# Decay totals of ten units taken from the last row of k's factor by small transfers, in an RWKV-6 and SwiGLU kernel

## The chip, the core and the metric

The kernel runs on one core of a Trainium2 chip. The metric is the device time of one execution in microseconds. Five engines work side by side, each through its own list of instructions in order: TensorE (PE in the profile, its weight loads shown as PEld), VectorE (DVE), ScalarE (ACT), GpSimd (POOL) and SyncE (SP), which here does nothing but issue transfers. Semaphores hold an instruction back until what it needs is there; whatever stands behind it on the same engine waits with it.

## What is computed

A recurrence over time with a state of 48 x 48 for each of 8 heads and 4 sequences, and a gated feed-forward layer on its output:

```python
for t in range(S):                                   # S = 768, D = 48
    cur = einsum('bhd,bhe->bhde', u * k[t], v[t])
    y[t] = einsum('bhd,bhde->bhe', r[t], state + cur)
    state = w[t][:, :, :, None] * state + einsum('bhd,bhe->bhde', k[t], v[t])
...
xn = x / sqrt(mean(x * x) + 1e-6) * rms_g            # x: 3072 tokens x 384
out = (silu(xn @ w_gate) * (xn @ w_val)) @ w_out     # 384 -> 1536 -> 384
```

All inputs are fp32, and so is the output of 3072 x 384.

## The kernel before

**Units.** Time is cut into six superblocks n = 0 to 5 of 128 steps (L), and in each the four sequences j = 0 to 3 are handled apart: a unit is a pair (n, j), 128 steps on the partitions and 8 heads x 48 values along a row. For a unit the recurrence becomes matrix products: with c the running sum of ln w within the superblock, r is multiplied by exp(c before the step), k by exp(-c after the step), the products r k (masked to earlier steps) give the part inside the superblock, and the state carries the rest. At the end of the unit the state is multiplied by the decay of the whole superblock, exp(the sum of ln w over all 128 steps). These numbers are called the decay totals here; there are 8 x 48 of them to a unit, and they are needed with the value index on the partitions, two heads to a column (`wcol`, 128 x 4 x 2).

**Steps of a unit that matter here**, each a function of the kernel:

- `ln` (ACT) makes ln w. `cs_mm` (PE) multiplies it by a triangular mask: the sums before each step go to a PSUM bank, `ps_au` or `ps_av`, columns 4 to 387. Four more matmuls (line 420) with ln w as the weights and a column of ones as the moving operand put the totals, already turned onto the partitions, into columns 0 to 3 of the same bank.
- `cs_add` (DVE) adds ln w for the sums after each step, into `ps_bu` or `ps_bv`.
- `exp_r` (ACT) takes the exponential of the first bank in place, totals included; `exp_k` (ACT) that of the second with the sign turned, into an SBUF tile `ek` (fp32, four buffers).
- `w_tot` (DVE, line 451) reads the four columns from PSUM and spreads them into `wcol`. `r_mul` (DVE) and `k_mul` (POOL, line 461, from superblock 2 on) multiply r and k by their factors into `rk`.
- `rk_tr` turns `rk` by a transposing transfer on SP's queue into `rkT`; `q_mm`, `y_mm` and `st_mm` (PE) use it; `st_new` (DVE, lines 536 and 537) adds the old state to the new products and multiplies by `wcol`.

Then come `x_add`, `x_sq`, `x_rstd`, `xn_mul`, `xn_pe` and `xn_out`, which normalise the 512 tokens of the superblock, and the feed-forward layer: twelve pairs `gate_mm` and `val_mm` (PE, line 626), each with `silu` (ACT) and `h_mul` (DVE, line 658), and four `o_mm` (PE, line 672) with `o_out` and `out_dma`. The feed-forward work of superblock n - 1 is interleaved with the recurrence of superblock n.

**What sets the order.** One table, `ORDER`, names every step of the program in one line of text, as function.n.j. The program is written out in that order, so each engine runs its share of the table strictly in that order, SP's transfers too. Buffers come in rings: PSUM in two banks `a` (gate, and the sums of `cs_mm`), two banks `b` (val, and `cs_add`) and four banks `q`. A `val_mm` therefore waits until the `h_mul` two places earlier has read its bank. SP issues, in one list, the loads of r, k, v and w, the transposing transfers of `rk_tr`, and the stores of the output.

Of the kernel before, what the change touches and what calls it, by code (L numbers as in the profile page):

```python
# [68 lines left out]
q_mask_o.2.3 st_mm.2.3 load_k.3.0 q_mask_o.2.2 q_mask_e.2.3 val_mm.1.11 q_mask_e.2.2 val_mm.1.10 bonus_v.2.3 y_mm.2.3
silu.1.11 y_mm.2.2 ln.3.0 h_mul.1.11 h_mul.1.10 x_rstd.2.1 x_add.2.2 ln.3.1 val_mm.1.8 ln.3.3 h_mul.1.8 cs_mm.3.0  # L70
load_r.3.0 x_sq.2.2 xn_mul.2.0 cast_v.3.2 cs_add.3.0 x_add.2.3 exp_k.3.0 x_sq.2.3 o_mm.1.0 cs_mm.3.1 xn_pe.2.0
exp_r.3.0 ln.3.2 x_rstd.2.2 o_mm.1.1 st_new.2.3 load_r.3.1 out_dma.0.3 w_tot.3.0 r_mul.3.0 xn_mul.2.1 k_mul.3.0
xn_mul.2.2 cs_add.3.1 exp_k.3.1 xn_pe.2.2 cs_mm.3.3 x_rstd.2.3 o_out.1.0 exp_r.3.1 bonus_mul.3.1 xn_out.2.2 xn_mul.2.3
o_mm.1.3 w_tot.3.1 xn_pe.2.3 o_out.1.1 cs_add.3.3 r_mul.3.1 load_k.3.2 load_r.3.3 xn_pe.2.1 xn_out.2.0 exp_r.3.3
exp_k.3.3 cs_mm.3.2 xn_out.2.3 o_mm.1.2 load_r.3.2 k_mul.3.1 w_tot.3.3 rk_tr.3.0 r_mul.3.3 cs_add.3.2 out_dma.1.0
xn_out.2.1 load_v.3.0 exp_r.3.2 gate_mm.2.5 exp_k.3.2 r_mul.3.2 w_tot.3.2 val_mm.2.0 gate_mm.2.0 bonus_mul.3.0
bonus_mul.3.2 k_mul.3.2 o_out.1.3 bonus_sum.3.0 silu.2.5 rk_tr.3.1 load_k.3.3 o_out.1.2 q_mm.3.0 silu.2.0 q_mask_e.3.0
val_mm.2.1 bonus_v.3.0 h_mul.2.0 gate_mm.2.1 load_w.4.1 load_v.3.1 load_k.4.3 st_mm.3.2 k_mul.3.3 q_copy_o.3.0
silu.2.1 rk_tr.3.2 load_v.4.0 rk_tr.3.3 val_mm.2.5 gate_mm.2.11 load_k.4.0 bonus_sum.3.1 cast_v.3.0 out_dma.1.1
load_v.3.3 load_w.5.2 q_mask_e.3.1 q_copy_o.3.1 gate_mm.2.2 silu.2.11 h_mul.2.5 val_mm.2.2 h_mul.2.1 load_w.4.0  # L80
# [12 lines left out]
rk_tr.4.0 xn_out.3.3 cs_add.4.3 load_k.5.3 o_mm.2.3 exp_r.4.3 xn_out.3.2 cs_add.4.2 bonus_mul.4.3 r_mul.4.3 w_tot.4.3
exp_k.4.3 exp_r.4.2 rk_tr.4.1 o_out.2.3 exp_k.4.2 load_v.4.2 val_mm.3.1 gate_mm.3.6 bonus_sum.4.0 k_mul.4.3 r_mul.4.2
st_mm.4.0 w_tot.4.2 load_r.5.3 load_k.5.0 val_mm.3.0 o_out.2.2 silu.3.6 st_new.4.0 k_mul.4.2 gate_mm.3.1 q_mm.4.0
cast_v.4.2 out_dma.2.2 bonus_sum.4.3 silu.3.1 gate_mm.3.0 q_copy_o.4.0 silu.3.0 h_mul.3.1 q_copy_o.4.1 gate_mm.3.3
val_mm.3.6 gate_mm.3.8 rk_tr.4.3 q_mask_e.4.0 h_mul.3.0 h_mul.3.6 st_mm.4.1 bonus_v.4.0 q_mask_e.4.1 q_mask_o.4.0
# [5 lines left out]
h_mul.3.10 silu.3.7 val_mm.3.2 gate_mm.3.5 h_mul.3.2 load_k.5.2 gate_mm.3.11 q_mask_o.4.2 y_mm.4.2 cast_v.4.3
xn_mul.4.1 val_mm.3.7 silu.3.5 bonus_mul.5.0 x_add.4.2 silu.3.11 ln.5.1 y_mm.4.3 h_mul.3.7 val_mm.3.11 x_add.4.3
load_v.5.3 x_sq.4.2 xn_tr.4.0 h_mul.3.11 x_sq.4.3 xn_tr.4.1 val_mm.3.5 st_mm.4.3 h_mul.3.5 x_rstd.4.2 cs_mm.5.1
cs_add.5.1 ln.5.2 xn_mul.4.2 x_rstd.4.3 o_mm.3.2 o_out.3.2 cs_mm.5.2 xn_tr.4.2 exp_k.5.1 cs_add.5.2 exp_r.5.1 o_mm.3.0
xn_mul.4.3 r_mul.5.1 ln.5.3 ln.5.0 xn_tr.4.3 cs_mm.5.0 st_new.4.3 exp_r.5.2 cast_v.5.3 exp_k.5.2 o_mm.3.1 out_dma.3.2
cs_add.5.0 out_dma.2.3 r_mul.5.2 exp_r.5.0 cs_mm.5.3 r_mul.5.0 st_mm.4.2 exp_k.5.0 cs_add.5.3 exp_r.5.3 o_mm.3.3
bonus_mul.5.1 xn_gain.4.0 xn_gain.4.2 xn_gain.4.1 k_mul.5.0 r_mul.5.3 exp_k.5.3 o_out.3.1 out_dma.2.1 o_out.3.0
gate_mm.4.0 val_mm.4.1 gate_mm.4.1 val_mm.4.0 bonus_sum.5.1 st_new.4.2 k_mul.5.1 k_mul.5.3 silu.4.0 load_v.5.0  # L110
rk_tr.5.0 silu.4.1 h_mul.4.0 gate_mm.4.3 gate_mm.4.2 rk_tr.5.1 silu.4.3 val_mm.4.2 bonus_sum.5.0 k_mul.5.2 gate_mm.4.4
silu.4.2 bonus_v.5.1 o_out.3.3 cast_v.5.0 h_mul.4.1 val_mm.4.3 q_mm.5.0 gate_mm.4.6 h_mul.4.2 bonus_mul.5.2 h_mul.4.3
# [19 lines left out]
def kernel(  # L132
# [18 lines left out]
    SB = B  # L151
# [573 lines left out]
```

## Time and profile before

| what | us |
|---|---|
| median of 3 runs | 201.49 |
| the three runs | 199.88, 201.49, 202.73 |
| the profiled execution, its own time | 200.28 |
| span of that execution in the profile | 198.6 |
| PE busy | 191.9 |
| DVE busy | 151.4 |
| ACT busy | 137.3 |
| POOL busy | 125.2 |

The times named below are microseconds from the start of the span. That execution took 1.7 us more than its span, which runs from the first instruction to the last. In rows of the timeline, the first number is the start, the second the duration, and a bracket tells of idle time before the row and of who ended it. An operation's line tells which function it comes from; `ps_au` and the like are PSUM banks. The granted clock of TensorE was 1.00 over the span.

### The profile page before, as it was taken

The page shows a single profiled execution, that of the slowest core. Times are in us where ns is not written, and L with a number is a line of the kernel's source. Part 1 is how long each engine was busy: PE and PEld are TensorE (multiplying, and loading weights), DVE is VectorE, ACT ScalarE, POOL GpSimd, SP SyncE. Part 2 cuts the span into 40 slices and gives each one's busy share as a digit, 9 for nine tenths or more (in the row PEclk, how much of TensorE's full clock was granted, in tenths as well). Part 3 has the DMA queues.
Part 4 walks back from the last instruction along what each step waited for, and adds up shares of the span by engine and source line. Part 5 has one row for each costly group of instructions (what it writes and reads, how often), then busy time and mean ns, then how long its engine had stood idle before and what let it go on. Part 6 is the DMA issues. An engine that isn't in the chain of part 4 may idle for free.

```text
span 198.6 us, 4409 instructions
## 1 busy us (share of the span) xinstructions
PE 191.9 (97%) x1577; PEld 113.9 (57%) x1577; DVE 151.4 (76%) x290; ACT 137.3 (69%) x279; POOL 125.2 (63%) x184
## 2 busy tenths in 40 slices
PE   7979998999999999999999999999999999999994
PEld 3556574465665565665556665556655565555562
DVE  6358989989998799987889989987887973173611
ACT  4399989579979569958559959399786683164300
POOL 5378993189399687899939899867686851000000
PEclk9999999999999999999999999999999999999999
DMA  6999999999999998999899879995499012032012
GB/s 153 268 235 176 183 220 203 214 180 211 179 195 224 206 196 196 236 198 207 193 195 225 188 171 204 204 183 107 138 187 208 0 25 60 6 112 83 0 59 101
DMA packets 121566, 32.41 MB, mean 163 GB/s; under 512 B 116420, under 2 KB 120392, under 8 KB 121544
## 3 DMA queue, kind: packets, MB, share of 16 engines
q1 hardware_dynamic: 119504, 28.58, 67.3%
q0 software_dynamic: 2032, 3.54, 10.0%
q8 instruction: 12, 0.20, 0.4%
q14 instruction: 10, 0.08, 0.1%
q10 hardware_dynamic: 8, 0.00, 0.0%
HBM read 25.96 MB, written 4.72 MB: 154 GB/s over the span
## 4 chain that ended last, share of the span: by engine, by line
PE 72%; SPq 18%; DMA 6%; POOL 2%; issue 1%; ACT 0%; POOLq 0%
SPq L248 16%; PE ps_av L626 10%; PE ps_bu L626 10%; PE ps_bv L626 10%; PE ps_au L626 10%; PE ps_qv L672 7%; PE ps_qz L672 7%; PE ps_qu L672 5%; PE ps_qx L672 4%; DMA wo_sb<-in_moe_w_out_dram 4%; DMA vt<-in_v_dram 3%; SPq L261 2%; PE ps_qz L502 1%; PE ps_qx L552 1%; PE ps_av L417 1%
## 5 line engine op out<-in xcount | busy, mean ns | idle before, releaser
L672 PEld LDWEIGHTS <-ht 128*128 128x128 bf16 x300 | 28.2, 98 | 17.0 <-issue 0.5
L626 PEld LDWEIGHTS <-wg_sb 128*128 128x128 bf16 x216 | 23.1, 114 | 19.7 <-DMA wg_sb<-in_moe_w_gate_dram 0.7
L626 PEld LDWEIGHTS <-wv_sb 128*128 128x128 bf16 x216 | 22.8, 114 | 19.0 <-DMA wv_sb<-in_moe_w_val_dram 1.0
L658 DVE TENSOR_TENSOR ht<-ps_bv,sg 128x512 bf16<-128x512 f32 x35 | 24.0, 686 | 10.1 <-PE ps_bv L626 9.2
L235 ACT ACTIVATE sg<-ps_av 128x512 bf16<-128x512 f32 x37 | 22.0, 595 | 12.3 <-PE ps_av L626 12.0
L626 PE MATMUL ps_av<-xnt,wg_sb 128*128 128x512 bf16 x111 | 30.1, 380 | 0.0
L626 PE MATMUL ps_bu<-xnt,wv_sb 128*128 128x512 bf16 x111 | 30.1, 380 | 0.0
L658 DVE TENSOR_TENSOR ht<-ps_bu,sg 128x512 bf16<-128x512 f32 x37 | 25.4, 686 | 6.0 <-PE ps_bu L626 5.2
L626 PE MATMUL ps_bv<-xnt,wv_sb 128*128 128x512 bf16 x105 | 28.5, 380 | 0.6 <-DMA wv_sb<-in_moe_w_val_dram 0.5
L626 PE MATMUL ps_au<-xnt,wg_sb 128*128 128x512 bf16 x105 | 28.5, 380 | 0.2 <-DMA wg_sb<-in_moe_w_gate_dram 0.2
L235 ACT ACTIVATE sg<-ps_au 128x512 bf16<-128x512 f32 x35 | 21.0, 599 | 10.8 <-PE ps_au L626 9.0
L467 POOL TENSOR_TENSOR ruk<-rt,kt 128x384 f32<-128x384 f32 x24 | 24.1, 1003 | 6.6 <-DMA kt<-in_k_dram 4.8
L468 POOL TENSOR_TENSOR ruk<-ruk,u_bc 128x384 f32<-128x384 f32 x24 | 24.4, 1017 | 1.9
L520 POOL TENSOR_SCALAR_AFFINE_SELECT qts<-qts 128x512 bf16<-128x512 bf16 x20 | 12.9, 653 | 15.1 <-ACT qts L513 14.6
L477 POOL TENSOR_TENSOR ydiag<-vt,diag 128x384 f32<-128x384 f32 x24 | 19.9, 833 | 1.0 <-DVE rk L461 0.5
L461 POOL TENSOR_TENSOR rk<-kt,ek 128x384 bf16<-128x384 f32 x16 | 15.9, 1007 | 2.3 <-ACT ek L235 2.3
L672 PE MATMUL ps_qv<-wo_sb,ht 128*128 128x384 bf16 (+1 forms) x96 | 15.0, 306 | 0.0
L672 PE MATMUL ps_qz<-wo_sb,ht 128*128 128x384 bf16 x84 | 14.8, 326 | 0.0
L233 ACT ACT_TABLE_LOAD x10 | 12.8, 1283 | 1.8 <-PEq L709 1.6
L235 ACT ACTIVATE lw<-wt 128x384 bf16<-128x384 f32 (+1 forms) x20 | 11.1, 578 | 4.2 <-DMA wt<-in_w_dram 4.1
L472 DVE TENSOR_REDUCE diag<-ruk 128x8 f32<-128x384 f32 x24 | 12.9, 543 | 0.7 <-POOL ruk L468 0.7
L585 ACT ACTIVATE xn<-xb,rstd 128x384 bf16<-128x384 f32 x20 | 11.8, 605 | 0.8 <-POOL rstd L580 0.8
(180 smaller groups left out, 373.6 us busy)
## 6 DMA issues: line engine op xcount, KB each, us to landing
rt<-in_r_dram SPq DMA_DIRECT2D x24, 192.0 KB, 3.9
kt<-in_k_dram SPq DMA_DIRECT2D x24, 192.0 KB, 4.0
vt<-in_v_dram SPq DMA_DIRECT2D x24, 192.0 KB, 3.7
out_dram<-ob SPq DMA_DIRECT2D x23, 192.0 KB, 2.3
wt<-in_w_dram SPq DMA_DIRECT2D x16, 192.0 KB, 4.0
wt<-in_w_dram SPq DMA_DIRECT2D x4, 384.0 KB, 4.4
wo_sb<-in_moe_w_out_dram POOLq DMA_DIRECT2D x3, 384.0 KB, 7.1
wg_sb<-in_moe_w_gate_dram POOLq DMA_DIRECT2D x1, 768.0 KB, 9.8
```

Source lines behind the costliest of these rows:

```text
L233: nc.scalar.preload_act_table_set(table_name)
L235: return nc.scalar.activation(**kw).ins
L248: dmas["load_" + which, n, j] = nc.sync.dma_start(out=inp[which, n, j], in_=t[j, :, n * L:(n + 1) * L, :].rearrange("h t d -> t h d")).ins
L461: eng.tensor_tensor(out=rk[:, n % 2, j, 1, :, 0:D], in0=inp["k", n, j], in1=bank["cs_k", n, j][:, 0:DM].rearrange("p (h d) -> p h d", h=H) ...
L467: nc.gpsimd.tensor_tensor(out=ruk[n, j], in0=inp["r", n, j], in1=inp["k", n, j], op=ALU.mult)
L468: nc.gpsimd.tensor_tensor(out=ruk[n, j], in0=ruk[n, j], in1=u_bc, op=ALU.mult)
L472: nc.vector.tensor_reduce(out=diag[n, j].rearrange("p h o -> p (h o)"), in_=ruk[n, j], axis=mybir.AxisListType.X, op=ALU.add)
L477: nc.gpsimd.tensor_tensor(out=ydiag[n, j], in0=inp["v", n, j], in1=diag[n, j].to_broadcast([128, H, D]), op=ALU.mult)
L520: nc.gpsimd.affine_select(out=qts[n, j][:, 1], in_=qts[n, j][:, 1], compare_op=ALU.is_gt, fill=0.0, base=0, pattern=[[0, NP], [1, 128]], c ...
L626: nc.tensor.matmul(ps[:, cols], lhsT=units(ws, c, f), rhs=xnt[n][:, c, cols], start=(first and c == 0), stop=(c == KC - 1))
L658: nc.vector.tensor_tensor(out=ht[n][:, f, :], in0=bank.pop(("v", n, f)), in1=bank.pop(("sg", n, f)), op=ALU.mult)
L672: nc.tensor.matmul(ps[:, cols], lhsT=ht[n][:, f, b * L:(b + 1) * L], rhs=wo_sb[:, f, cols], start=(f == 0), stop=(f == FC - 1))
```

## The change

For ten of the twelve units of superblocks 2, 3 and 4 (all but 2.1 and 4.1) the decay totals are no longer made by `cs_mm`. The last row of `ek`, on partition 127, holds exp(-c) after the last step, the reciprocal of the totals. Two transfers on SP's queue (`tot_dma`, 48 pieces of 16 bytes each) carry that row to a tile `tcol` with the value index on the partitions; DVE takes the reciprocal and multiplies it into `wcol`. So that the pieces are 16 bytes long, `exp_k` of these units writes `ek` with the four head pairs innermost, values 16 bytes apart, and `k_mul` reads it so.

```diff
+    TOT_DMA = sel("30 31 32 33 40 42 43 20 22 23")
...
-    def tot(n):
+    def tot(n, j):
...
-        return NP if n < NSB - 1 else 0
+        return NP if n < NSB - 1 and (n, j) not in TOT_DMA else 0
...
     def exp_k(n, j):
         ps = bank["cs_k", n, j][:, 0:DM]
+        if (n, j) in TOT_DMA:
+            bank["cs_k", n, j] = pt.tile([128, DM], FP32, name="ek", bufs=NE)
+            act(LN_EXP, out=bank["cs_k", n, j].rearrange("p (i d q) -> p q i d", i=2, d=D),
+                in_=ps.rearrange("p (q i d) -> p q i d", i=2, d=D), func=AF.Exp, scale=-1.0)
+            return
...
+    tcol = small.tile([128, 2, SB, NP], FP32, name="tcol")
+    nc.vector.memset(tcol, 1.0)
+
+    def tot_dma(n, j):
+        row = bank["cs_k", n, j][L - 1:L, :].rearrange("o (i d q) -> o i d q", i=2, d=D)
+        for i in range(2):
+            nc.sync.dma_start(out=tcol[i * PD:i * PD + D, n % 2, j, :], in_=row[:, i])
+
     def w_tot(n, j):
+        if (n, j) in TOT_DMA:
+            wcol[n, j] = small.tile([128, NP, 2], FP32, name="wcol", bufs=8)
+            rec = tcol[:, n % 2, j]
+            nc.vector.reciprocal(rec, rec)
+            nc.vector.tensor_tensor(out=wcol[n, j], in0=rec.unsqueeze(2).to_broadcast([128, NP, 2]),
+                                    in1=bc_mid(half_of, NP), op=ALU.mult)
+            return
...
     def k_mul(n, j):
+        if (n, j) in TOT_DMA:
+            nc.gpsimd.tensor_tensor(out=rk[:, n % 2, j, 1, :, 0:D].rearrange("p (q i) d -> p q i d", i=2),
+                                    in0=inp["k", n, j].rearrange("p (q i) d -> p q i d", i=2),
+                                    in1=bank["cs_k", n, j].rearrange("p (i d q) -> p q i d", i=2, d=D), op=ALU.mult)
+            return
```

In `ORDER` each `w_tot` of the ten units moves from beside its `r_mul` to just ahead of its `st_new`, and each unit gets a `tot_dma` some way behind its `exp_k`; nothing else of the table changes places:

```diff
-gate_mm.2.3 load_v.4.1 silu.2.2 q_mask_o.3.0 cast_v.3.1 load_r.4.1 bonus_sum.3.2 h_mul.2.2 bonus_v.3.1 gate_mm.2.6
-val_mm.2.3 y_mm.3.0 st_new.3.2 st_mm.3.0 silu.2.3 gate_mm.2.4 h_mul.2.3 silu.2.6 q_mask_o.3.1 st_new.3.0 st_mm.3.1
+cast_v.3.1 load_r.4.1 bonus_sum.3.2 h_mul.2.2 bonus_v.3.1 gate_mm.2.6 val_mm.2.3 y_mm.3.0 w_tot.3.2 st_new.3.2
+st_mm.3.0 silu.2.3 gate_mm.2.4 h_mul.2.3 silu.2.6 q_mask_o.3.1 w_tot.3.0 st_new.3.0 st_mm.3.1 silu.2.4 x_add.3.0
```

The change in DVE's list, at the states of units 3.2, 3.0 and 3.1 (`ht` is `h_mul`, `diag` is `bonus_sum`, `xb` is `x_add`, `st` is `st_new`). Before:

```order
159 L472 TENSOR_REDUCE diag<-ruk 128x8
160 L658 TENSOR_TENSOR ht<-ps_bu,sg 128x512
161 L536 TENSOR_TENSOR ps_qv<-ps_qv,st 128x384
162 L537 TENSOR_TENSOR st<-ps_qv,wcol 128x384
163 L658 TENSOR_TENSOR ht<-ps_bv,sg 128x512
164 L536 TENSOR_TENSOR ps_qz<-ps_qz,st 128x384
165 L537 TENSOR_TENSOR st<-ps_qz,wcol 128x384
```

The same stretch of DVE's list after the change:

```order
159 L500 TENSOR_REDUCE diag<-ruk 128x8
160 L686 TENSOR_TENSOR ht<-ps_bu,sg 128x512
161 L462 RECIPROCAL tcol<-tcol 128x4
162 L463 TENSOR_TENSOR wcol<-tcol,half_of 128x8
163 L564 TENSOR_TENSOR ps_qv<-ps_qv,st 128x384
164 L565 TENSOR_TENSOR st<-ps_qv,wcol 128x384
165 L686 TENSOR_TENSOR ht<-ps_bv,sg 128x512
166 L462 RECIPROCAL tcol<-tcol 128x4
167 L463 TENSOR_TENSOR wcol<-tcol,half_of 128x8
168 L564 TENSOR_TENSOR ps_qz<-ps_qz,st 128x384
169 L565 TENSOR_TENSOR st<-ps_qz,wcol 128x384
```

A reciprocal and a product now stand ahead of each `st_new`, and both operands of the product, `tcol` and `half_of`, are SBUF tiles, where the old product read PSUM.

SP's list where superblock 3 gives its totals (`rkT` is `rk_tr`, `kt`, `vt` and `wt` are loads of k, v and w). Before, from `rk_tr.3.1` on:

```order
58 L489 DMA_TRANSPOSE rkT<-rk 128x8x128
59 L248 DMA kt<-in_k_dram 128x8x48
60 L261 DMA wt<-in_w_dram 128x8x48
61 L248 DMA vt<-in_v_dram 128x8x48
62 L248 DMA kt<-in_k_dram 128x8x48
63 L489 DMA_TRANSPOSE rkT<-rk 128x8x128
64 L248 DMA vt<-in_v_dram 128x8x48
```

After the change, from the same `rk_tr.3.1`:

```order
62 L517 DMA_TRANSPOSE rkT<-rk 128x8x128
63 L456 DMA tcol<-ek 48x1x4 x4
64 L251 DMA kt<-in_k_dram 128x8x48
65 L264 DMA wt<-in_w_dram 128x8x48
66 L456 DMA tcol<-ek 48x1x4 x2
67 L251 DMA vt<-in_v_dram 128x8x48
68 L251 DMA kt<-in_k_dram 128x8x48
69 L517 DMA_TRANSPOSE rkT<-rk 128x8x128
70 L251 DMA vt<-in_v_dram 128x8x48
```

Four transfers of totals (units 3.1 and 3.2) stand ahead of the load of k for unit 3.3, and two more (unit 3.3) ahead of the load of v for unit 3.1 and all that follows it.

More of the change, by code (lines that the diff above doesn't have):

```diff
@@ L71 @@
[L71 to L80, printed above, removed]
@@ L81 @@
-gate_mm.2.3 load_v.4.1 silu.2.2 q_mask_o.3.0 cast_v.3.1 load_r.4.1 bonus_sum.3.2 h_mul.2.2 bonus_v.3.1 gate_mm.2.6
-val_mm.2.3 y_mm.3.0 st_new.3.2 st_mm.3.0 silu.2.3 gate_mm.2.4 h_mul.2.3 silu.2.6 q_mask_o.3.1 st_new.3.0 st_mm.3.1
-silu.2.4 x_add.3.0 load_k.4.1 gate_mm.2.7 val_mm.2.4 x_sq.3.0 gate_mm.2.10 out_dma.1.2 cast_v.4.0 st_new.3.1
-val_mm.2.6 q_mm.3.2 h_mul.2.4 bonus_mul.3.3 h_mul.2.6 silu.2.7 val_mm.2.7 val_mm.2.10 load_w.4.3 x_rstd.3.0 silu.2.10
+xn_out.1.1 exp_k.2.0 tot_dma.2.0 out_dma.0.0 load_k.2.2 exp_r.2.1 load_v.2.0 ln.2.2 k_mul.2.0 ln.2.3 w_tot.2.1
@@ new lines @@
+r_mul.2.1 cs_mm.2.2 xn_pe.1.3 cs_mm.2.3 exp_k.2.1 xn_out.1.2 cs_add.2.2 k_mul.2.1 cs_add.2.3 cast_v.2.1 exp_r.2.2
+exp_r.2.3 rk_tr.2.1 xn_out.1.3 o_mm.0.3 exp_k.2.3 o_out.0.1 r_mul.2.2 bonus_mul.2.1 gate_mm.1.7 val_mm.1.7 exp_k.2.2
+load_k.2.3 st_mm.2.1 rk_tr.2.0 bonus_sum.2.0 r_mul.2.3 gate_mm.1.1 load_v.2.2 tot_dma.2.2 st_new.2.1 k_mul.2.2
+silu.1.7 bonus_mul.2.2 silu.1.1 bonus_sum.2.1 val_mm.1.1 h_mul.1.7 gate_mm.1.6 silu.1.6 bonus_v.2.1 gate_mm.1.5
+cast_v.2.0 k_mul.2.3 silu.1.5 rk_tr.2.2 val_mm.1.5 load_w.3.3 o_out.0.2 h_mul.1.1 gate_mm.1.3 gate_mm.1.0 val_mm.1.0
@@ L93 @@
[L93 to L97, printed above, removed]
@@ L103 @@
[L103 to L107, printed above, removed]
@@ L108 @@
[L108 to L112, printed above, removed]
@@ new lines @@
+xn_mul.3.1 o_out.2.0 x_rstd.3.2 xn_mul.3.2 ln.4.2 exp_r.4.1 load_r.5.1 tot_dma.4.0 x_rstd.3.3 k_mul.4.0 xn_out.3.0
+load_r.4.3 out_dma.1.3 bonus_sum.4.1 xn_pe.3.1 xn_out.3.1 ln.4.3 exp_k.4.1 bonus_mul.4.2 xn_mul.3.3 r_mul.4.1
+k_mul.4.1 w_tot.4.1 out_dma.2.0 o_mm.2.1 cs_mm.4.2 xn_pe.3.3 bonus_mul.4.0 cast_v.4.1 xn_pe.3.2 o_out.2.1 cs_mm.4.3
+bonus_sum.4.2 rk_tr.4.0 xn_out.3.3 cs_add.4.3 load_k.5.3 o_mm.2.3 exp_r.4.3 xn_out.3.2 cs_add.4.2 bonus_mul.4.3
+r_mul.4.3 exp_k.4.3 exp_r.4.2 rk_tr.4.1 o_out.2.3 exp_k.4.2 load_v.4.2 tot_dma.4.3 val_mm.3.1 gate_mm.3.6
@@ new lines @@
+h_mul.3.7 val_mm.3.11 x_add.4.3 load_v.5.3 x_sq.4.2 xn_tr.4.0 h_mul.3.11 x_sq.4.3 xn_tr.4.1 val_mm.3.5 st_mm.4.3
+h_mul.3.5 x_rstd.4.2 cs_mm.5.1 cs_add.5.1 ln.5.2 xn_mul.4.2 x_rstd.4.3 o_mm.3.2 o_out.3.2 cs_mm.5.2 xn_tr.4.2
+exp_k.5.1 cs_add.5.2 exp_r.5.1 o_mm.3.0 xn_mul.4.3 r_mul.5.1 ln.5.3 ln.5.0 xn_tr.4.3 cs_mm.5.0 w_tot.4.3 st_new.4.3
+exp_r.5.2 cast_v.5.3 exp_k.5.2 o_mm.3.1 out_dma.3.2 cs_add.5.0 out_dma.2.3 r_mul.5.2 exp_r.5.0 cs_mm.5.3 r_mul.5.0
+st_mm.4.2 exp_k.5.0 cs_add.5.3 exp_r.5.3 o_mm.3.3 bonus_mul.5.1 xn_gain.4.0 xn_gain.4.2 xn_gain.4.1 k_mul.5.0
@@ new lines @@
+r_mul.5.3 exp_k.5.3 o_out.3.1 out_dma.2.1 o_out.3.0 gate_mm.4.0 val_mm.4.1 gate_mm.4.1 val_mm.4.0 bonus_sum.5.1
+w_tot.4.2 st_new.4.2 k_mul.5.1 k_mul.5.3 silu.4.0 load_v.5.0 rk_tr.5.0 silu.4.1 h_mul.4.0 gate_mm.4.3 gate_mm.4.2
+rk_tr.5.1 silu.4.3 val_mm.4.2 bonus_sum.5.0 k_mul.5.2 gate_mm.4.4 silu.4.2 bonus_v.5.1 o_out.3.3 cast_v.5.0 h_mul.4.1
+val_mm.4.3 q_mm.5.0 gate_mm.4.6 h_mul.4.2 bonus_mul.5.2 h_mul.4.3 silu.4.4 q_copy_o.5.0 q_mask_o.5.0 gate_mm.4.5
+out_dma.3.1 q_mask_e.5.0 y_mm.5.0 silu.4.6 q_copy_o.5.1 bonus_v.5.0 rk_tr.5.2 load_v.5.2 silu.4.5 rk_tr.5.3 x_add.5.0
```

100 lines of the change are left out of this document (54 added, 46 removed).

## The prediction

> **What bounds the kernel now.** I read the page first, for the span and the busy time of each engine:
>
> ```profile
> span 198.6 us, 4409 instructions
> PE 191.9 (97%) x1577; PEld 113.9 (57%) x1577; DVE 151.4 (76%) x290; ACT 137.3 (69%) x279; POOL 125.2 (63%) x184
> ```
>
> Then the chain that ended last (start, duration, what). Its last link off PE ends here, and from here to the last ACT copy it stays on PE:
>
> ```profile
> 53.16 0.81 PE ps_qx L672 x4
> ...
> 194.63 1.00 PE ps_qv L672 x12
> ```
>
> So from 53 us on, time comes off only where PE has less to do, and is added wherever PE must wait for the first time. How far the others are from holding it shows in busy time by stages (us, then for each engine its busy time):
>
> ```profile
> 70.00:80.00 10.00, 10.00 (x110) 6.06 (x108) 9.75 (x18) 7.79 (x17) 8.33 (x14) 1.00 0.92 195
> 90.00:100.00 10.00, 10.00 (x81) 5.64 (x80) 8.54 (x17) 7.04 (x13) 9.14 (x13) 1.00 1.00 211
> 100.00:110.00 10.00, 10.00 (x106) 6.04 (x105) 9.26 (x18) 7.85 (x17) 6.41 (x11) 1.00 1.02 211
> ```
>
> The columns are PE, PEld, DVE, ACT, POOL. PE is never idle, DVE is at 85 to 98%, POOL at 91% in one stage. This is a schedule in which three engines are nearly full, so new work on DVE or POOL is paid for wherever it exceeds the little room ahead of PE.
>
> **What PE is spared.** PE's timeline around one unit:
>
> ```profile
> 58.47 0.33 PE L417 MATMUL ps_au<-lw,mask_lt 128*128 128x384 bf16 x1
> 58.63 0.24 PE L420 MATMUL ps_au<-ones_col,lw 128*128 128x1 bf16 x4
> 58.74 0.33 PE L596 MATMUL ps_qx<-ident,xn 128*128 128x128 bf16 x3
> ```
>
> The durations overlap, so the price is the distance of starts: 58.74 - 58.63 = 0.11 us for four matmuls with their weight loads. Ten units give 1.1 us, all on the path: the first term is **-1.1 us**, 0.5% of the time, and no more can be gained here. That `exp_r` reads 384 columns in place of 388 and that `tcol` is set once at the start I cost at nothing; ACT loses four columns in 388, and the set stands before the first totals, where DVE waits for ACT.
>
> **What DVE gets.** The old product is short:
>
> ```profile
> L451 DVE TENSOR_TENSOR wcol<-ps_au,half_of x6: 155/156/166, 57.4 to 119.5; 128x8 f32<-128x8 f32 x6
> ```
>
> The reciprocal I price like it, 0.16 us (the trace has none; 0.1 to 0.3). The product needs the reciprocal, so the two don't overlap: about 0.3 us ahead of each `st_new`. That is the price if nothing stands in the way. But the new product reads two SBUF tiles. The trace has such products, the `r_mul` of superblock 1, whose factor lies in SBUF (`er`), beside those with a PSUM factor (min/median/max ns):
>
> ```profile
> L455 DVE TENSOR_TENSOR rk<-rt,ps_av x10: 542/544/554, 11.9 to 145.7; 128x384 bf16<-128x384 f32 x10
> L455 DVE TENSOR_TENSOR rk<-rt,er x4: 541/1004/2060, 24.1 to 39.4; 128x384 bf16<-128x384 f32 x4
> ```
>
> One of the slow ones, and what POOL did then:
>
> ```profile
> 24.15 1.35 DVE L455 TENSOR_TENSOR rk<-rt,er 128x384 bf16<-128x384 f32 x1
> 23.88 1.20 POOL L468 TENSOR_TENSOR ruk<-ruk,u_bc 128x384 f32<-128x384 f32 x1
> ```
>
> POOL's operation ends at 25.08, and 0.42 us later DVE's ends, about its undisturbed length. So DVE waited for POOL's operation to end, and all behind it waited too. The Trainium skill states this as a rule, page "SBUF — State Buffer", section "Who interferes with whom": a VectorE instruction with two SBUF inputs contends with a GpSimd instruction that reads SBUF, and the one that comes second is held for all of the other. The rows above agree; that a product of 8 columns waits as one of 384 does is what no row of before shows.
>
> I take it that it does, and read from POOL's rows what each wait would be. Two stages decide. The first is superblock 2:
>
> ```profile
> 74.07 0.56 DVE L536 TENSOR_TENSOR ps_qu<-ps_qu,st 128x384 f32<-128x384 f32 x1
> 73.54 1.01 POOL L468 TENSOR_TENSOR ruk<-ruk,u_bc 128x384 f32<-128x384 f32 x1
> 78.53 0.68 DVE L658 TENSOR_TENSOR ht<-ps_bv,sg 128x512 bf16<-128x512 f32 x1
> 79.53 0.82 PE L626 MATMUL ps_bv<-xnt,wv_sb 128*128 128x512 bf16 x3
> ```
>
> The totals of 2.2 come at 74.07; the product waits until 74.55 and ends 0.16 later, 0.6 us in all. With 0.3 for unit 2.0, less the 0.25 us that DVE idles in this stage, DVE is 0.65 late at 79.21, when it gives `ps_bv` back; PE has 0.32 us of room there. PE loses **0.3 us**. The second is superblock 3:
>
> ```profile
> 97.25 0.56 DVE L536 TENSOR_TENSOR ps_qv<-ps_qv,st 128x384 f32<-128x384 f32 x1
> ...
> 101.79 0.68 DVE L658 TENSOR_TENSOR ht<-ps_bu,sg 128x512 bf16<-128x512 f32 x1
> ```
>
> ```profile
> 97.20 1.02 POOL L467 TENSOR_TENSOR ruk<-rt,kt 128x384 f32<-128x384 f32 x1
> 98.30 1.00 POOL L468 TENSOR_TENSOR ruk<-ruk,u_bc 128x384 f32<-128x384 f32 x1
> 101.55 0.19 POOL L579 TENSOR_SCALAR rstd<-rstd 128x1 f32<-128x1 f32 x1 [2.25 <-ACT junk L570]
> ```
>
> ```profile
> 102.92 0.84 PE L626 MATMUL ps_bu<-xnt,wv_sb 128*128 128x512 bf16 x3
> ```
>
> The totals of 3.2 wait from 97.25 to 98.22 and end 1.1 us late, those of 3.0 and 3.1 add 0.3 each: 1.7 us, less some 0.2 that DVE idles between. The `h_mul` at 101.79 must be done (102.47) when PE takes `ps_bu` at 102.92, 0.45 us of room: PE loses **1.0 us**. The other five (2.3, 3.3 and superblock 4) I put at the same price for less tight places, **0.5 us** together. The old products that go give back 10 x 0.08 us of DVE's list, at other places, where I count nothing. Bounds of this term: 0 if the small product never waits and the 0.3 us hide, 3.5 if each waits for a whole operation of 1 us. I take the middle, which the rows at hand give: **+1.8 us**.
>
> **What POOL and ACT get.** `k_mul` now reads `ek` 16 bytes apart, which no row shows:
>
> ```profile
> L461 POOL TENSOR_TENSOR rk<-kt,ek x16: 995/1002/1097, 57.9 to 147.1; 128x384 bf16<-128x384 f32 x16
> L381 POOL CAST vb<-vt 128x384 bf16<-128x384 f32 x16 | 8.1, 507 | 0.1
> ```
>
> Below it costs nothing, above a further pass over one operand, as a cast makes it: 1.0 to 1.5 us each; nothing in it can gain. I take 1.25. Superblock 3 is the tight place, for POOL runs without a gap from 82.24 to 99.30:
>
> ```profile
> 91.18 1.00 POOL L461 TENSOR_TENSOR rk<-kt,ek 128x384 bf16<-128x384 f32 x1
> 93.62 0.33 PE L530 MATMUL ps_qv<-vb,rk 128*128 128x96 bf16 x4
> ```
>
> PE takes this `k_mul` (3.2) 1.44 us after it ends. Three of them have come by then, 0.75 us late at my price: hidden, **0 us**, and 0.1 at the upper end. The gap of 2.25 us at 101.55 takes up the rest. The Trainium skill speaks against the change here: page "GPSIMD Engine Reference", section "Performance pitfalls for Q7 kernels", says that reading SBUF with a step above 8 bytes costs about half as much again for each element. By that estimate `k_mul` takes 1.5 us and the sum grows by 0.1. `exp_k` writes with the same step; its nearest rows are ACT's own operations over 384 elements, 0.47 to 0.60 us, so 0 to 0.13 us each, hidden in ACT's 20 to 30% of idle time.
>
> **What SP gets.** Twenty issues, and two waits for ACT with loads behind them:
>
> ```profile
> 87.18 1.24 SPq L489 DMA_TRANSPOSE rkT<-rk  x1
> 88.46 0.58 SPq L248 DMA_DIRECT2D kt<-in_k_dram  x1
> ...
> 93.49 0.58 SPq L248 DMA_DIRECT2D vt<-in_v_dram  x1
> 89.58 0.49 ACT L235 ACTIVATE ek<-ps_bv 128x384 f32<-128x384 f32 x1
> L687 SPq DMA_DIRECT2D out_dram<-ob x25: 332/422/2581, 58.0 to 196.0; - x25
> DMA to landing us min/median/max: 1.6/2.3/4.8
> ```
>
> An issue I price like a store's median, 0.42 us. The transfers of 3.1 go out from 88.42 to 89.26, those of 3.2 wait for `exp_k.3.2` until 90.07 and are out at 90.9; the load of k at 88.46 goes 2.4 us later, that of v at 93.49 (for unit 4.0, whose cast on POOL comes at 96.73) up to 3.3 later. POOL then waits some 2 to 3 us ahead of 99.3, about its gap of 2.25 at 101.55: **0 us** on the path. `w_tot.3.2` has the shortest lead: issued by 90.9 and landed 2.3 us later, 93.2, it is wanted at 97.25; at the slowest landing, 95.7, still in time.
>
> **The sum.** -1.1 + 1.8 = +0.7 us on an execution of 200.28, 201.0. The median of the runs lies 1.2 above that execution, so I forecast **202.2 us**. The runs before spread from 199.88 to 202.73, so about 2%, 4 us, is what a measurement of this kernel can tell from no change.
>
> **The rivals.** *The gain is kept* (0.20): the small product does not wait, or DVE's lateness hides. For it: DVE's wait is seen only on products of 384 columns; against it: 0.32 and 0.45 us of room. 201.5 - 1.1 = 200.4.
>
> *POOL becomes late* (0.22), the slower side: the strided read costs more than a pass. It decides from 1.0 + 1.44/3 = 1.48 us for a `k_mul`. If it doubles to 2.0, the `k_mul` of 3.2 is 3.0 late, 1.6 beyond PE's room; superblocks 2 and 4, with three each, I put at 0.8 apiece. With longer operations of POOL DVE waits longer too. 0.7 + 3.2 gives 205.4, and 206 with DVE's part. For it: POOL at 91%; against it: the cast's row.
>
> *SP's list is the bound* (0.12): late loads pass their 2.4 to 3.3 us on to superblock 4, since the transfer engines run at shares of 1.00 to 1.02 and cannot catch up; some 2 us beyond the gap reach PE: 204.2. Against it: no transfer but the weights holds PE before.
>
> **How the numbers follow.** My own case has 0.42, 200.5 to 204.2 with its bounds and the spread of a median; 0.04 is left for others. The range, 199.4 to 206.5, reaches from a kept gain in a fast set of runs to a late POOL. Slower by over 2% (205.5): 0.13 of the POOL rival, 0.04 of SP's, 0.05 of mine, 0.03 of others, 0.25. Faster by over 2% (197.5) needs more than PE is spared: 0.03. Within: 0.72.
>
> **What would show it.** PE's matmuls of one column down from 48 to 8. Products into `wcol` from `tcol` that last from 0.16 to 1 us and end with POOL's operations; waits of PE or ACT for `h_mul` near 79 and 102 us. `k_mul` at 1.0 to 1.5 us; at 2.0 POOL's rival holds. If the new products all take 0.16 us, my main term falls. If waits for `kt` or `vt` appear on POOL with more than 3 us, SP's rival holds.

## The result, and the profile after

| | before | after |
|---|---|---|
| median, us (six runs each) | 200.64 | 208.05 |
| lowest and highest | 199.88, 202.73 | 207.63, 209.53 |
| ratio, with its 95% interval | | 1.0385 (1.0352 to 1.0418) |
| profiled execution, its own time and span | 200.28, 198.6 | 208.39, 206.7 |

The change makes the kernel 3.9% slower, 7.7 us by the ratio. The forecast was 202.2 with a range up to 206.5, so it was wrong, though the sign of its sum was right. (Here and below a median is over all runs of a kernel, and a ratio over those that are not in a slower state that some executions of any kernel fall into.) The page of after opens so:

```profile
span 206.7 us, 4357 instructions
PE 193.3 (94%) x1517; PEld 113.0 (55%) x1537; DVE 155.9 (75%) x301; ACT 140.9 (68%) x279; POOL 127.1 (61%) x184
```

PE's share of the span falls from 97 to 94%: outside its busy time lie 13.4 us, where there were 6.7. (That the busy time is 1.4 us longer, with forty matmuls gone, says little, since the ends of matmuls are modelled.) The waits of PE (waiting line, who released it, us in all, times, longest) say where. Before had no wait of more than 0.5 us on PE for another engine behind the loading stage; after has these among others:

```profile
PE ps_bv L654 <- ACT ek L238: 1.5, 1, 1.5
PE ps_qz L530 <- DMA rkT<-rk: 0.9, 1, 0.9
PE ps_qx L532 <- DVE st L565: 0.6, 2, 0.4
```

They name three producers, no one of which is the cause by itself. What stands behind them shows one step further back. POOL's waits in after:

```profile
POOL ruk L495 <- DMA kt<-in_k_dram: 7.6, 3, 4.4
...
POOL rk L484 <- DMA kt<-in_k_dram: 3.3, 2, 2.8
```

Before, POOL waited 4.8 us for k in all, 4.4 of it in one piece (a wait that after has too), and never ahead of `k_mul`. The longest PE wait can be followed back through the timelines of after. POOL, for `bonus_mul.4.1`:

```profile
114.03 0.99 POOL L495 TENSOR_TENSOR ruk<-rt,kt 128x384 f32<-128x384 f32 x1 [2.57 <-DMA kt<-in_k_dram]
```

DVE, where `bonus_sum.4.2` waits for a later product of POOL and `cs_add` stands behind it:

```profile
122.06 0.55 DVE L500 TENSOR_REDUCE diag<-ruk 128x8 f32<-128x384 f32 x1 [2.04 <-POOL ruk L496]
```

and ACT, where `exp_r.4.3` and `exp_k.4.3` come late behind that `cs_add`:

```profile
123.58 0.47 ACT L238 ACTIVATE ps_av<-ps_av 128x384 f32<-128x384 f32 x1 [2.54 <-DVE ps_bv L428]
123.97 0.86 ACT L238 ACTIVATE ek<-ps_bv 128x384 f32<-128x384 f32 x1
```

The load of k for unit 4.1 that POOL waits for was issued at 102.20 before the change and at 110.09 after it. That is SP's list. Around the totals of superblock 3 it now reads (SP's own timeline of after; `tcol` are the new transfers, `x4` four of them):

```profile
92.97 2.44 SPq L456 DMA_DIRECT2D tcol<-ek  x4
95.45 0.59 SPq L251 DMA_DIRECT2D kt<-in_k_dram  x1
96.09 0.57 SPq L264 DMA_DIRECT2D wt<-in_w_dram  x1
96.70 1.46 SPq L456 DMA_DIRECT2D tcol<-ek  x2
98.21 0.58 SPq L251 DMA_DIRECT2D vt<-in_v_dram  x1
```

There is no gap above 0.1 us in it, and the load of k (3.3) that stood at 88.46 before stands at 95.45, 7.0 us later, where the prediction had 2.4. The stretch of the list from the load of r for unit 2.3 (57.32 before, 58.16 after) to that for unit 5.1 (108.44 and 115.80) takes 51.1 us before and 57.6 after. The windows around it, first before, then after (PE, PEld, DVE, ACT, POOL busy, granted clock, share of the transfer engines, GB/s):

```profile
57.00:111.00 54.00, 54.00 (x475) 32.20 (x473) 47.84 (x96) 40.76 (x84) 44.74 (x64) 1.00 1.00 207
```

```profile
57.00:118.00 61.00, 57.64 (x458) 33.33 (x465) 53.05 (x110) 45.50 (x89) 47.13 (x66) 1.00 0.93 181
```

Before the change the share of the transfer engines is 1.00 over the window; after it they have idle time (0.93; 0.59 between 90 and 100 us, where six of the issues stand), though loads are late. Something ahead of them holds the loads back.

The operations themselves, by tile, in after (ns: lowest, median, highest). `exp_k` is L238; ten of its twenty operations are strided, and each of its two rows mixes both kinds:

```profile
L456 SPq DMA_DIRECT2D tcol<-ek x20: 523/585/966, 58.8 to 128.0; - x20
L238 ACT ACTIVATE ek<-ps_bu x10: 467/488/902, 16.5 to 153.3; 128x384 f32<-128x384 f32 x10
L238 ACT ACTIVATE ek<-ps_bv x10: 467/853/888, 25.3 to 151.1; 128x384 f32<-128x384 f32 x10
L484 POOL TENSOR_TENSOR rk<-kt,ek x10: 1183/1194/1206, 58.7 to 128.6; 128x384 bf16<-128x384 f32 x10
```

And the new product of DVE, by its line:

```profile
L463 DVE TENSOR_TENSOR wcol<-tcol,half_of x10: 168/456/890, 71.0 to 155.3; 128x8 f32<-128x8 f32 x10
```

### The profile page after: what moved, and what is told of

Read it like the earlier page. It is cut to its first block, busy times and chain, and to the rows that moved or that the text cites. A ratio compares the mean times of both kernels' runs of the same rounds, so it can differ in the third digit from the quotient of the medians.

```text
span 206.7 us, 4357 instructions
## 1 busy us (share of the span) xinstructions
PE 193.3 (94%) x1517; PEld 113.0 (55%) x1537; DVE 155.9 (75%) x301; ACT 140.9 (68%) x279; POOL 127.1 (61%) x184
## 4 chain that ended last, share of the span: by engine, by line
PE 54%; SPq 10%; DMA 10%; DVE 8%; POOL 7%; issue 4%; ACT 4%; DVEq 0%; POOLq 0%; ACTq 0%
PE ps_au L654 9%; PE ps_av L654 9%; PE ps_bv L654 9%; PE ps_bu L654 8%; SPq L251 6%; DMA rt<-in_r_dram 5%; DMA kt<-in_k_dram 4%; SPq L264 3%; PE ps_qv L700 3%; PE ps_qu L700 3%; POOL ruk L496 2%; POOL ruk L495 2%; PE ps_qz L700 2%; PE ps_qx L700 2%; DMA rkT<-rk 2%
## 5 line engine op out<-in xcount | busy, mean ns | idle before, releaser
L238 ACT ACTIVATE sg<-ps_av 128x512 bf16<-128x512 f32 x37 | 22.0, 595 | 12.7 <-PE ps_av L654 10.8
L654 PE MATMUL ps_bu<-xnt,wv_sb 128*128 128x512 bf16 x102 | 29.2, 379 | 0.7 <-DVE ht L686 0.2
L238 ACT ACTIVATE sg<-ps_au 128x512 bf16<-128x512 f32 x35 | 21.0, 599 | 11.7 <-PE ps_au L654 7.7
L484 POOL TENSOR_TENSOR rk<-kt,ek 128x384 bf16<-128x384 f32 x10 | 11.9, 1195 | 4.0 <-DMA kt<-in_k_dram 3.3
L238 ACT ACTIVATE lw<-wt 128x384 bf16<-128x384 f32 (+1 forms) x20 | 11.1, 578 | 4.2 <-DMA wt<-in_w_dram 4.1
```

What stands on the lines that cost most here:

```text
L238: return nc.scalar.activation(**kw).ins
L484: nc.gpsimd.tensor_tensor(out=rk[:, n % 2, j, 1, :, 0:D].rearrange("p (q i) d -> p q i d", i=2), in0=inp["k", n, j].rearrange("p (q i) d - ...
L654: nc.tensor.matmul(ps[:, cols], lhsT=units(ws, c, f), rhs=xnt[n][:, c, cols], start=(first and c == 0), stop=(c == KC - 1))
```

## The experiments

Three theories for the 7.7 us. A: SP's list is the bound, and the twenty issues delay the loads. B: the strided `exp_k`, 0.85 to 0.90 us in place of 0.48, holds ACT and then PE. C: DVE's products, held by POOL, are dearer than priced. Ratios are to the kernel before, run beside each experiment, with their 95% intervals; 0.01 is 2.0 us.

### One part taken from the changed kernel

**Without the transfers:** every `tot_dma` struck from `ORDER`.

> The changed kernel without its twenty transfers of totals (the totals of the ten units stay 1.0, so the states decay wrongly; everything else is issued as it was). Theory A, SP's list is the bound: the loads behind the transfers come 2 to 10 us late and starve POOL; without the transfers most of the 7.4 us goes and the time is 201 to 203.5. Theory B, the strided exp_k on ACT (0.88 in place of 0.48 us) carries the loss: the time stays at 206 or more. Theory C, DVE's held products carry it: 205 or more, since the products stay.

Measured 203.58, ratio 1.0124 (1.0095 to 1.0153). Of 3.85 points 2.6 go with the transfers, 5.2 us. The time is 0.1 us above A's range, and well below what B and C gave. A holds for two thirds of the loss; the remaining 2.5 us have other causes.

**Without the stride:**

```diff
-            act(LN_EXP, out=bank["cs_k", n, j].rearrange("p (i d q) -> p q i d", i=2, d=D),
-                in_=ps.rearrange("p (q i d) -> p q i d", i=2, d=D), func=AF.Exp, scale=-1.0)
+            act(LN_EXP, out=bank["cs_k", n, j], in_=ps, func=AF.Exp, scale=-1.0)
```

> The changed kernel with ek written and read without a stride; the transfers keep their place, number and pieces (16 bytes, 48 each), so they carry other values of the row and the totals are wrong. Theory A: at most 2 us go, 206 to 208. Theory B: 202 to 204, since exp_k is back at 0.48 us and k_mul at 1.0.

Measured 207.27, ratio 1.0292 (1.0222 to 1.0362): some 1.9 us less than the change, 0.3 to 3.4 by the intervals, as A had it. B falls as the main cause.

**Without a product of two SBUF tiles:** two reciprocals, one per half of the partitions, in place of a reciprocal and a product, written into a tile of zeros.

```diff
-            nc.vector.reciprocal(rec, rec)
-            nc.vector.tensor_tensor(out=wcol[n, j], in0=rec.unsqueeze(2).to_broadcast([128, NP, 2]),
-                                    in1=bc_mid(half_of, NP), op=ALU.mult)
+            for i in range(2):
+                p = slice(i * PD, i * PD + PD)
+                nc.vector.reciprocal(wcol[n, j][p, :, i], tcol[p, n % 2, j])
```

> The changed kernel with the product of two SBUF tiles replaced: two reciprocals, one for each half of the partitions, write straight into a tile of zeros, so no operation of the totals reads two SBUF tiles. Same output. Theory C, held products: 10 x 0.3 us of waiting at the median leaves DVE and the time falls by 1.5 to 3, to 205 to 206.5. Theories A and B: 207 to 208, since DVE's lateness lies beside the wait for the loads.

Measured 207.15, ratio 1.0304 (1.0206 to 1.0402). The interval reaches past the changed kernel's own ratio: beside late loads the price of the products can't be told from none. It is measured by itself further down.

### One part added to the kernel before

**The transfers alone:** `tot_dma` at the change's places, totals by matmuls as before.

> The kernel before (totals by matmuls, ek without stride) with the twenty transfers put into SP's list at the places where the changed kernel has them; nobody reads what they carry. Theory A: 204 to 206.5, most of the loss with none of the rest. Theories B and C: 200 to 202.5, the transfers hide.

Measured 207.21, ratio 1.0279 (1.0215 to 1.0343), above the range that A gave. The transfers by themselves cost about what they cost in the changed kernel. In the profiled execution it is a load of r that comes late first: DVE waits 2.85 us for it up to 86.56, and PE 1.61 us behind DVE up to 87.17.

**The same from a source that is ready:**

```diff
-        row = bank["cs_k", n, j][L - 1:L, :].rearrange("o (i d q) -> o i d q", i=2, d=D)
+        row = u_bc[L - 1:L].rearrange("p h d -> p (h d)").rearrange("o (i d q) -> o i d q", i=2, d=D)
```

> The kernel before with the twenty transfers at the same places of SP's list, but their source is a row of u that has been ready since the start: no transfer waits for ACT, and nobody reads what they carry. Theory A1, the issues themselves fill a list that has no idle time (20 x 0.59 = 11.7 us against some 7 us of idle time between 57 and 122 us): 204.5 to 207.5, like the run whose source is ek (207.2). Theory A2, the wait for exp_k with the loads behind it: 200.5 to 202.5.

Measured 205.81, ratio 1.0256 (1.0194 to 1.0317): A1. No transfer waits for ACT here, and the loss is the same within the intervals. The wait for `exp_k`, which the prediction had named, is not where most of the loss lies.

**Ten issues in place of twenty:** one of each unit's two transfers, from the ready source.

> The kernel before with ten transfers in place of twenty, one for each of the ten units, at the same places, from a source that is ready. If every issue adds its 0.59 us to a full list, half the loss of the twenty (205.8): 202.5 to 204. If the idle time of the list (some 7 us between 57 and 122) takes the first issues up, less than 1 us: 200 to 201.3.

Measured 202.19, ratio 1.0083 (1.0048 to 1.0118), 1.7 us, between the two ranges: neither nothing, as idle time in the list would make it, nor quite half of 5.1.

**Twenty issues of one piece:** `out=tcol[i * PD:i * PD + 1, ...], in_=row[:, i, 0:1]`, 16 bytes each.

> The kernel before with twenty transfers from a ready source, each of one piece of 16 bytes in place of 48. If the price lies in the issue, whatever it carries: 204.5 to 206.5, like the twenty of 48 pieces (205.8). If it lies in the pieces (their descriptors, or the transfer engines): 201 to 203.

Measured 205.17, ratio 1.0211 (1.0162 to 1.0261): the price lies in the issue, not in what it carries. The tile's row in that kernel agrees; an issue takes 576 ns with one piece, 590 with 48:

```profile
L455 SPq DMA_DIRECT2D tcol<-u_bc x20: 567/576/748, 58.2 to 125.9; - x20
```

**The stride alone** (strided `exp_k` and `k_mul`, totals by matmuls):

> The kernel before with the strided ek alone: exp_k of the ten units writes 16 bytes apart, k_mul reads so; totals by matmuls, no transfers. Same output. By the prediction (exp_k 0 to 0.13 us more, k_mul 1.25, all hidden): 200.5 to 201.3. With exp_k at 0.88 and k_mul at 1.19, as the changed kernel's trace has them, ACT and POOL have 0.6 us more for each unit: 201.3 to 202.5. Theory B: 203 or more.

Measured 201.63, ratio 1.0079 (1.0046 to 1.0112), 1.6 us (0.9 to 2.2): ACT's 0.39 and POOL's 0.19 us per unit are not all hidden, and which of the two costs isn't shown. The profiled execution, 203.74, puts the cost at the lower end. Its `h_mul` stand 2.7 us behind those of before at 40 us already, ahead of the first strided operation at 59.11, and 3.5 us from 126 us on, so that 0.8 us were added where the strided operations are.

**The matmuls alone taken out,** and with the reciprocal and product put back:

> The changed kernel without transfers, without the stride of ek and without the reciprocal and product (a constant 1 stands for the totals of the ten units, so the states decay wrongly): only the forty matmuls of one column and ten old products are gone. By the prediction's first term, 1.1 us of PE's path: 199.5 to 200.3 against 200.9 of before, ratio 0.993 to 0.997. Rival: the next engine takes the gain, ratio 0.998 to 1.002.

> The run with the matmuls alone removed (199.7), and DVE's reciprocal and product of two SBUF tiles put back for each of the ten units; no transfers, no stride, and the totals are 1, so the states decay wrongly. By the prediction's second term, held products delay PE by 1.8 us: 201.5, ratio to before 1.002 to 1.009. Rival, DVE's lateness hides where no load is late: ratio 0.996 to 1.000.

Measured 199.70, ratio 0.9970 (0.9947 to 0.9993), and 201.80, ratio 1.0081 (1.0042 to 1.0120). The gain is 0.6 us, the products cost 1.1 points, 2.2 us (1.3 to 3.1). In the second kernel the product still waits for POOL, with no load late:

```profile
L461 DVE TENSOR_TENSOR wcol<-tcol,half_of x10: 166/248/820, 69.8 to 148.4; 128x8 f32<-128x8 f32 x10
```

The longest of them, beside POOL's operation:

```profile
119.63 1.00 POOL L494 TENSOR_TENSOR ruk<-ruk,u_bc 128x384 f32<-128x384 f32 x1
119.83 0.82 DVE L461 TENSOR_TENSOR wcol<-tcol,half_of 128x8 f32<-128x8 f32 x1
```

POOL's ends at 120.63, the product at 120.65. All seven that took 0.2 us or more end so, within 0.03 us behind an operation of POOL; the other three took 0.17. The ten were held for 1.8 us in all, the sum of their times less ten times 0.17. PE waits 0.6 us for DVE behind the loading stage; in the kernel without the products it has no such wait. What the 2.2 us owe to the holding, and what to the 0.3 us that each reciprocal and product take without it, was not measured apart.

### Where the issues stand

**Issued by ACT:** `nc.scalar.dma_start` in place of `nc.sync.dma_start`.

> The changed kernel with the twenty transfers issued by ACT instead of SP, at the same places of the order. Theory A1: SP's list is as before, and the time falls to 203 to 205, less if an issue costs ACT little, more (205 to 207) if ACT is held for 0.59 us by each as SP is. Theories B and C, stride and held products: 206.5 or more whatever queue issues them.

Measured 209.53, ratio 1.0465 (1.0435 to 1.0495), slower still, and beyond every range that A1 gave; by the number alone B and C could be right. The waits say otherwise. The loads are in time again (POOL's waits for k are back to 5.9 us, none ahead of `k_mul`), but now ACT stands while it issues, and PE waits for ACT. ACT's timeline, the work ahead of an issue, two issues, and the work behind them:

```profile
63.38 0.88 ACT L238 ACTIVATE ek<-ps_bv 128x384 f32<-128x384 f32 x1
64.29 1.35 ACTq L456 DMA_DIRECT2D tcol<-ek  x2
65.67 1.28 ACT L236 ACT_TABLE_LOAD   x1 [1.41 <-issue]
```

Not every pair costs so much: from 89.20 to 90.52 ACT's operations follow one another without a pause beside two issues. PE's longest waits in that kernel:

```profile
PE ps_au L654 <- ACT sg L238: 2.8, 2, 1.8
```

The longer of these two, 1.8 us up to 67.61, is for the `silu` behind the rows above. So the price follows the engine that issues. It doesn't lie in the transfers.

**At later places of SP's list.** In this kernel the transfer of 2.3 stands behind its use, so the state of that unit is not decayed.

> The changed kernel with the transfers at later places of SP's list, behind the loads that they stood ahead of and, in superblocks 3 and 4, ahead of transposes for which SP waited before the change (3.1, 3.2 and 3.3 behind load_k.4.3, 4.2 and 4.3 behind load_k.5.0, 4.0 behind load_r.4.3, 2.0, 2.2 and 2.3 further down as well). If the loss comes from which loads are behind the transfers: 204.5 to 206.8. If from the sum of issue times alone: 207.3 to 208.5.

Measured 209.05, ratio 1.0441 (1.0388 to 1.0494), above both ranges. No gain: putting the loads first does not help, for other loads are then behind. In its profiled execution the `h_mul` that before has at 106.77 is 3.0 us late, where the changed kernel's is 4.1; at the one of 121.90 both are 7.0 to 7.1 late. POOL waits 4.4 us for a load of v up to 104.48, and 2.8 for one of k up to 113.98.

**Fewer issues, the same bytes:** w loaded for two units at a time, in the changed kernel and in the one before.

```diff
-            o = inp["w", n, j].rearrange("p (b h d) -> p b h d", b=2, h=H)[:, j % 2]
-            src = w[j, :, n * L:(n + 1) * L, :].rearrange("h t d -> t h d")
+            o = inp["w", n, j].rearrange("p (b h d) -> p (b h) d", b=2, h=H)
+            src = w[i:i + 2, :, n * L:(n + 1) * L, :].rearrange("b h t d -> t (b h) d")
```

> The changed kernel, with the loads of w of superblocks 2 to 5 issued two units at a time, as one transfer of 384 KB at the place of the first in place of two of 192 KB: eight issues fewer in SP's list (six of them between 57 and 141 us), the same bytes. Same output. If issue time in SP's list binds, 6 x 0.59 = 3.5 us of list come back: 204.5 to 207. If the bytes of the transfer engines bind (their share is near 1), 207.5 to 209.

> The kernel before with the same paired loads of w: eight issues fewer, none added. If the list of before has just enough idle time, PE has nothing to gain: ratio 0.995 to 1.003. If the list already holds PE up a little, ratio 0.985 to 0.995.

Measured 208.21, ratio 1.0408 (1.0357 to 1.0459), and 201.46, ratio 1.0059 (1.0035 to 1.0084). The first lies where the bound by bytes had put it (207.5 to 209), not where the bound by issues had; the second misses both of its ranges, and is a little slower. Its trace has no loss where the issues were taken away: from 70 us on its `h_mul` keep their distance to those of before, 0.38 to 0.39 us. Taking issues away gains nothing. SP's rows tell why. The changed kernel, then the one with paired w, up to the load of k for 4.1:

```profile
105.15 2.06 SPq L264 DMA_DIRECT2D wt<-in_w_dram  x2
107.26 0.68 SPq L251 DMA_DIRECT2D vt<-in_v_dram  x1
107.98 2.07 SPq L251 DMA_DIRECT2D rt<-in_r_dram  x1
110.09 0.76 SPq L251 DMA_DIRECT2D kt<-in_k_dram  x1
```

```profile
104.75 0.74 SPq L266 DMA_DIRECT2D wt<-in_w_dram  x1
105.54 2.33 SPq L251 DMA_DIRECT2D vt<-in_v_dram  x1
107.92 2.21 SPq L251 DMA_DIRECT2D rt<-in_r_dram  x1
110.17 0.63 SPq L251 DMA_DIRECT2D kt<-in_k_dram  x1
```

One issue fewer, and the next takes 2.33 in place of 0.68 us: k is issued at the same time. Among loads, then, a second limit stands right behind SP's own. That it is the transfer engines taking their bytes is the likely reading (in the changed kernel their share is 1.12 from 100 to 112 us, in this run of loads), but the trace names no releaser for those longer issues.

**Twenty issues among the loads, or behind the transposes:** if that second limit gives an issue cover, the place should decide.

> The kernel before with the same twenty transfers from a ready source (48 pieces of 16 bytes, nobody reads them), but each directly behind a load in the two runs of loads, 8 of them between 70 and 82 us and 12 between 97 and 110. If SP there waits anyway for the transfer engines to take its loads (issues of 0.7 to 2.6 us in the trace of before), an issue of 0.58 takes the place of waiting and the time is 200.3 to 202.5. If an issue costs its time wherever it stands: 204.5 to 206.5, like the twenty at the change's places (205.8).

> The same twenty transfers, two directly behind each of the transposes of 2.0 to 2.3, 3.0 to 3.3, 4.0 and 4.1, where SP's list is held by issue time and not by the transfer engines. If the place decides: at least the loss of the change's places, 205.5 to 208.5. If only their number decides: 204.5 to 206.5, and the same as the run with the transfers among the loads.

Measured 205.49, ratio 1.0238 (1.0172 to 1.0304), and 207.94, ratio 1.0324 (1.0251 to 1.0396). Among loads they are not free. The second lies in the range for a place that decides, but the two intervals overlap, so whether the place matters stays open. SP's list of the kernel before at that place:

```profile
97.45 2.21 SPq L261 DMA_DIRECT2D wt<-in_w_dram  x2
99.70 0.68 SPq L248 DMA_DIRECT2D vt<-in_v_dram  x1
100.43 1.73 SPq L248 DMA_DIRECT2D rt<-in_r_dram  x1
102.20 0.78 SPq L248 DMA_DIRECT2D kt<-in_k_dram  x1
103.08 0.59 SPq L687 DMA_DIRECT2D out_dram<-ob  x1
```

and with the transfers among the loads:

```profile
101.31 0.76 SPq L265 DMA_DIRECT2D wt<-in_w_dram  x1
102.11 2.17 SPq L458 DMA_DIRECT2D tcol<-u_bc  x1
104.33 0.58 SPq L265 DMA_DIRECT2D wt<-in_w_dram  x1
104.96 0.58 SPq L458 DMA_DIRECT2D tcol<-u_bc  x1
...
108.11 0.58 SPq L252 DMA_DIRECT2D kt<-in_k_dram  x1
108.73 0.59 SPq L458 DMA_DIRECT2D tcol<-u_bc  x1
109.42 0.53 SPq L710 DMA_DIRECT2D out_dram<-ob  x1
```

From the load of w to the store it was 5.63 us and is 8.11: five transfers cost 0.5 us of list each. The first waits 2.17 us, as a load did before; from then on every issue takes its 0.53 to 0.59 with no gap above 0.1 us, and SP is the limit: the share of the transfer engines is 0.72 between 105 and 110 us, where before has 0.98 to 1.02 through its run of loads (95 to 111). So the list of before stood close to both limits at once: without more issues the loads wait in their queue, with more of them SP itself can't send fast enough. Adding issues costs, and removing some gains nothing.

No version that computes the totals was found to beat the kernel before. With the transfers, the stride and the products all gone, only 0.6 us are to be had.

## Why the prediction was wrong, point by point

The parts measured alone, as points of the ratio: matmuls -0.3, products +1.1, stride +0.8, transfers from `ek` +2.8, together +4.4 against +3.85 measured. They overlap a little, but nothing large is left out.

- **PE, -1.1 us.** Measured 0.6 (0.1 to 1.1): right in sign, at the edge in size.
- **DVE, +1.8 us.** Measured 2.2 (1.3 to 3.1). The mechanism held: a product of 8 columns took from 168 to 890 ns, the long ones ended with POOL's operations, and 0.6 us of PE's waits name DVE. The rival that it would not wait falls. The places did not hold: in the kernel with the products alone, 1.4 of the 1.8 us of holding fell in superblock 4, which with 2.3 and 3.3 was priced at 0.5 in all, and the product of 3.2, expected to wait 0.97 us, waited 0.07. That the sum came out near is partly luck.
- **POOL, `k_mul` 1.25 us, hidden.** It takes 1.194 against 1.000 in the units that keep the old form, 19% more, well below the 1.48 at which the rival of a late POOL would have decided. By the estimate from the Trainium skill's page "GPSIMD Engine Reference", section "Performance pitfalls for Q7 kernels", it would have been 1.5; the measurement decides against it here. POOL became late all the same, for want of loads.
- **ACT, `exp_k` 0 to 0.13 us more, hidden.** This step failed. It was bounded by ACT's other operations over 384 elements, none of which writes single values apart; the strided write takes 0.85 to 0.90 in place of 0.48. With `k_mul` it costs 1.6 us by itself (0.9 to 2.2), and the prediction had 0 for both.
- **SP, 0 us.** This is the step that failed most, by over 5 us. Three things were wrong in it. The issue was priced at a store's median, 0.42, where it takes 0.585, and with the gap to the next 0.63. Then each delay was counted by itself, 2.4 us for the load of k, 3.3 for that of v. But SP's list had almost no room: between 57 and 111 us of before it makes 54 issues, and its rows show four pauses above 0.3 us, 3.1 us in all, the longest this one of 1.06 us ahead of the transpose at 83.90:

```profile
80.84 2.00 SPq L248 DMA_DIRECT2D rt<-in_r_dram  x2
83.90 1.36 SPq L489 DMA_TRANSPOSE rkT<-rk  x1
```

  In after a single such pause, of 0.43 us, is left between 57 and 119 us. So the delays of superblock 2 were still there in superblock 3 and added up: 7.0 us at the load of k (3.3), 7.6 at that of v (4.0). Twelve of the issues stand ahead of that load of k; an estimate from the rows, twelve times 0.63 us, less 1.9 us of pauses used up, plus 0.8 us that the list was late ahead of the first of them, gives 6.5 of the 7.0. And POOL's gap of 2.25 us at 101.55 could cover one late load, but not three in a row: in after POOL waits 2.8 us ahead of `k_mul.3.3`, 1.5 ahead of a cast and 2.57 at 114.03.
- **The rivals.** "SP's list is the bound" named what happened, with late loads passed on to superblock 4, at 0.12 and 204.2. It gave another reason: that the transfer engines, at shares of 1.00 to 1.02, could not catch up. Their share fell to 0.93, and the issues held the loads. Its sign, waits of POOL for `kt` of more than 3 us, could not tell, for before has 4.8 us of them; what tells is that `k_mul` now waits for its load. What spoke against it, that no transfer but the weights holds PE before, was no argument: a transfer may be one issue from holding an engine.

## What to carry to other kernels

The issuing engine has a capacity too, and the page's busy times don't show it: lay its timeline out, subtract the pauses, and set the added issues times their price against what is left over the whole stretch, not at each place alone. A transfer of 16 bytes cost its issuer as much here as one of 192 KB that its queue took at once, so replacing 0.11 us of matmuls by two issues needs an engine with 1.2 us to spare. And a layout made for the transfer is paid for by whoever writes and reads it, each time.

## What the runs showed of the hardware

- An ACT operation on 384 fp32 values that writes them 16 bytes apart took 0.85 to 0.90 us, with a contiguous output 0.47 to 0.52.
- A DVE product of 128 x 8 with both operands in SBUF took 0.17 us by itself and up to 0.89 beside POOL; in the kernel with the products alone the seven long ones ended within 0.03 us behind an operation of POOL.
- An issue of totals took 0.58 to 0.59 us on SP at the median, whether of one piece or of 48, and a load of 192 KB no more where its queue had room (0.57 to 0.59; directly behind a store mostly 0.42 to 0.44). On ACT it took 0.51 to 0.8 us.
- In the profiled execution of the kernel before with the transfers (207.13 us), PE stood for 1.61 us up to 87.17, and some 1.7 us later the granted clock fell to 0.50 for about 3.4 us. Its windows (the clock is the column ahead of the last two):

```profile
84.00:86.00 2.00, 1.55 (x12) 0.76 (x9) 0.00 (x0) 1.16 (x3) 0.85 (x1) 1.00 1.00 235
86.00:88.00 2.00, 0.41 (x5) 0.29 (x6) 1.44 (x4) 0.38 (x1) 1.65 (x4) 1.00 0.59 119
88.00:90.00 2.00, 1.90 (x9) 1.05 (x9) 1.98 (x6) 2.00 (x6) 1.92 (x3) 0.72 0.77 148
90.00:92.00 2.00, 2.00 (x12) 1.25 (x11) 0.38 (x2) 0.18 (x1) 1.92 (x3) 0.50 1.17 277
```

  Another execution of that kernel had a mean clock of 1.00 and took 207.29 us, so its loss doesn't hang on that.
